# Attention then MoE on one core: V cast in smaller pieces, weight sums halved and earlier, four stores reordered

## Chip, core and metric

One core of a Trainium2 chip. The metric is the device time of one execution in microseconds (us); before the change the median of five runs is 349.75, the lowest 347.26 and the highest 356.05.

The core has five engines with instruction queues of their own: TensorE (PE in the profile, with its weight loads as PEld), VectorE (DVE), ScalarE (ACT), GpSimd (POOL) and SyncE (SP, which here only issues DMAs). An engine works through its queue in order, and instructions wait for each other across engines by semaphores.

## The reference

Two operators, one after the other. Attention over 8 batches, 8 heads, 576 positions and 64 columns a head, causal by blocks of 64; then a two-layer feed-forward network over the 8 x 576 = 4608 rows, with swish and a slope for each hidden column. All inputs and the output are float32.

```python
def _attn_ref(q, k, v):                       # (8, 8, 576, 64) each
    scores = 1.0 / np.sqrt(64) * np.matmul(q, k.transpose(0, 1, 3, 2))
    mask = (pos[:, None] // 64) >= (pos[None, :] // 64)
    scores = np.where(mask, scores, -1e9)
    scores = scores - np.max(scores, axis=-1, keepdims=True)
    attn = np.exp(scores)
    attn = attn / (np.sum(attn, axis=-1, keepdims=True) + 1e-09)
    return np.matmul(attn, v)

def _moe_ref(x, w_in, w_out, beta):           # (4608, 512), (512, 2048), (2048, 512), (2048,)
    h = x @ w_in
    g = h * (1.0 / (1.0 + np.exp(-beta * h)))
    return g @ w_out

x = attn_out.transpose(0, 2, 1, 3).reshape(4608, 512)
```

## The kernel before

**A plan made at build time.** The kernel first lists its operations (`P.op`) with an estimated duration, the operations it depends on (`deps`), the buffers it uses (`tiles`) and a priority (`prio`, the lower the sooner). A list scheduler (`Plan.schedule`, L81) then walks through an estimated time: whenever an engine is free, it takes the ready operation with the lowest priority, gives it its buffers, and writes it into that engine's queue. The queues are fixed from then on; on the chip only the semaphore waits decide when the instructions start. A dependency in `deps` counts with its latency: the later operation is not planned before the earlier has ended, and a wait is written where another engine, or a DMA, is awaited. `after` is weaker: the later operation may not be planned before the earlier is, and no wait comes of it (L207). Since buffers are given out in the order of the plan, one changed estimate or one weaker dependency can move many operations after it, on every engine.

**Attention.** The work is cut into 32 units, one for each batch b and pair of heads c (`u` = 4b + c). For a unit:

- q and k are loaded by SyncE into staging buffers `ST`, cast to bf16 by GpSimd (`QKn`, L647) and turned: for batches 0 and 1 by TensorE, from batch 2 on by one DMA transpose for two units, issued by SyncE (L654), into `QKT`.
- V of a whole batch is loaded by SyncE into `Vs` (128 rows x 2560 columns of float32) and cast to bf16 by GpSimd into `Vn` (L558). There are two `Vs` buffers. For batch 0 the cast is made in pieces of two heads, from batch 1 on in one instruction of 128x2560 (`range(h0, h1, 2 if b == 0 else 8)`). The second `Vs` buffer, like two of the six `ST` buffers, lies in the space `OV`, which later holds the sums below; batches 2 and later use the first only.
- TensorE makes the scores in two groups of six matmuls (L685), into pairs of PSUM banks; ScalarE takes their exponential (L699, three of 128x1024 a unit and a small one), 30 matmuls of 128x65 form the weighted sum and its denominator (L737), in a pair of banks from the same pool (banks 0 to 3 from batch 1 on).
- VectorE divides (L756, into `xq`). The result is turned into `xT`, the input of the network: for batches 0 to 4 by TensorE (L781) with a copy (L789), from batch 5 on by DMA transposes that SyncE issues (L769).

SyncE's queue thus holds all loads of q, k and V and, from batch 2 on, the transposes.

**The network.** The 4608 rows are worked in 9 chunks `r` of 512. For each of the 16 blocks `j` of hidden columns, H (four matmuls of 512 columns, L946), the tanh on ScalarE (L956) and the product on VectorE (L960) make block j of `gT`. "H j5 of chunk 1" is such a group. Chunk 0 then multiplies with `w_out` plainly (L982; its 16 groups are the list `plain`). `w_out` is loaded by GpSimd's queue in four parts (`wout`, L494), after the V load of batch 1.

Chunks 1 to 8 use seven products in place of eight (L817 to L933). `gT` is cut into quarters G(a, b), a for the rows and b for the hidden blocks, `w_out` into quarters b. VectorE makes, for each chunk, the sums of quarters of `gT`, each in two halves of 128x1024 (`comb`, L846):

```
S3 = G00 - G10 (SW[3])    S1 = G10 + G11 (in place of G10)
S2 = S1 - G00  (SW[2])    S4 = G01 - S2  (in place of G01)
```

and once, at the start of chunk 1, the sums of `w_out` (`weights`, L823): `TW3 = b3 - b1`, `TW1 = b1 - b0` (in place of b1), `TW2 = b3 - TW1`, `TW4 = b2 - TW2`, each one instruction of 128x2048 (L828). TW2, TW3, TW4 and S2, S3 lie in `OV`, so they wait until the early `ST` and `Vs` buffers there have been read (`early`). A product (`prod`, L879) is two steps of eight matmuls of 256 columns; in the order of the code: p1 = G00 b0, p2 = G01 b2, p6 = S2 TW2, p7 = S3 TW3, p5 = S1 TW1, p3 = S4 b3, p4 = G11 TW4. The second step of a product depends on the first. Products add up in three PSUM banks Z, W and Y. `evac` brings them out: ScalarE copies a bank with the factor 0.5 (L893: z1, u2, tt, c12), VectorE adds a bank to such a copy (L896: c11, c22, c21, into `oz`, `ot`, `ou`). Each of the four quarters of the result is then written to memory by a DMA that ScalarE issues (`store`, L903), right where its result is listed; such a store stands in ScalarE's queue and holds what is behind it until its result is there.

In the span, H groups and products of one chunk, and score groups, weighted sums and turns of later units, take turns on TensorE; the priorities (`pr`, L425; L888; L951) spread the units over the chunks.

Of the kernel before, what the change touches and what calls it, by code (L numbers as in the profile page):

```python
# [5 lines left out]
ALU = mybir.AluOpType  # L6
# [25 lines left out]
class Op:  # L32
    def __init__(self, engs, dur, lat, emit, deps, tiles, prio, mode, dma, xfer):
        self.xfer = xfer
        self.engs, self.dur, self.lat, self.emit = engs, dur, lat, emit
        self.deps, self.tiles, self.prio, self.mode, self.dma = list(deps), tiles, prio, mode, dma
        self.eng = None
        self.start = self.end = None
        self.order = None
        self.need = False  # L40
        self.tick = None
        self.after = None
        self.lazy = False
        self.pkt = 22.0
        self.fill = 0


class Plan:
# [32 lines left out]
    def schedule(self):  # L81
# [85 lines left out]
        while nsched < len(self.ops) - len(fill) or pend or rings["H"] or rings["S"] or late:  # L167
# [26 lines left out]
            while progress:  # L194
                progress = False
                for e in engs:
# [4 lines left out]
                    for o in pool:  # L201
                        if e not in o.engs:
                            continue
                        if o.ready + slack > now + 1e-9:
                            heapq.heappush(events, o.ready + slack)
                            continue
# [144 lines left out]
def bass_blockwise_causal_attn__then__act_swish_beta_kernel(  # L351
# [10 lines left out]
    with es:  # L362
# [58 lines left out]
        def dve_t(n):  # L421
            return (n + 125) / 0.96
# [97 lines left out]
        for b in range(B):  # L520
# [4 lines left out]
            for h0, h1, e, tt in PARTS[b]:  # L525
# [27 lines left out]
                n = 5 if 4 in tt else len(tt)  # L553
                for g0 in range(h0, h1, 2 if b == 0 else 8):
                    g1 = g0 + 2 if b == 0 else h1

                    def fw(g, e, ts=ts, t=t, g0=g0, g1=g1, n=n):
                        return g.tensor_copy(Vn[t.slot][:, 0:n, g0:g1, 0:64], Vs[ts.slot][:, 0:n, g0:g1, :])  # L558

                    o = P.op("POOL", 60 + 60 * n * (g1 - g0), fw, deps=[*vs, *ones, *vzero], tiles=[ts, t],  # L560
                             prio=4 * b + 0.5 - (38.5 - 5 * (h0 > 0)) * (b < 1))
                    for h in range(g0, g1, 2):
                        load[4 * b + h // 2] = [o]
# [259 lines left out]
        def weights():  # L823
            old = plain + wout + [o for t in early for o in t.users]
            b = [quad(w_out, 0, 0), quad(w_out, 0, 1), quad(w_out, 1, 0), quad(w_out, 1, 1)]
            for k, o, x, y, of in ((3, TW[3], b[3], b[1], []), (1, b[1], b[1], b[0], []),
                                   (2, TW[2], b[3], b[1], [1]), (4, TW[4], b[2], TW[2], [2])):
                tw[k] = P.op("DVE", dve_t(1024), mk(lambda g, o=o, x=x, y=y: g.tensor_tensor(o, x, y, ALU.subtract)),  # L828
                             deps=old + list(tw.values()), prio=0.6)
                tw[k].same = [tw[i] for i in of]  # L830

        def fast(r, row, tg, gs):
# [41 lines left out]
            def prod(ps, fa, fb, deps, tiles, first, last):  # L874
                z = []
                for w in range(2):
                    def fp(g, e, w=w):
                        for j in range(HJ):
# [7 lines left out]
                    n = HJ * mm(HM)  # L886
                    z.append(P.op("PE", n, fp, deps=deps + z, tiles=[ps, tg, *tiles], lat=n + 170, mode="full",
                                  prio=1000 + 100 * r + (16 + 0.1 * k if fin or k < 2 else 103 + 16 / 12 * (k - 2))))  # L888
                return z

# [10 lines left out]

            def store(to, a, b, x):
                return P.op("ACT", 500, lambda g, e: [g.dma_start(  # L903
                    out_rows(a, b), ost[to.slot][:].rearrange("p (w n) -> p w n", w=2))],
                    deps=[x], tiles=[to], xfer=900, dma=["d_ost", to], prio=-1)

            Z, W, Y = P.tile("P1"), P.tile("P1"), P.tile("P1")
# [6 lines left out]
            c11 = evac(W, oz, p2 + [z1], add=oz)  # L914
            store(oz, 0, 0, c11)
            for i in range(NP):
# [3 lines left out]
                SS[4].append(o)  # L920
            p6 = prod(Z, lambda: SW[2], lambda: TW[2], SS[2] + [tw[2], z1], [t2], False, False)
            u2 = evac(Z, ou, p6)
            p7 = prod(Y, lambda: SW[3], lambda: TW[3], SS[3] + [tw[3]], [t3], True, False)
            p5 = prod(Z, lambda: G(1, 0), lambda: quad(w_out, 0, 1), SS[1] + [tw[1], u2], [], False, False)
            tt = evac(Z, ot, p5)
            c22 = evac(Y, ot, p7 + [tt], add=ot)
            store(ot, 1, 1, c22)
            p3 = prod(Z, lambda: G(0, 1), lambda: quad(w_out, 1, 1), SS[4] + [tt] + wh, [], False, True)
            c12 = evac(Z, oc, p3)
            store(oc, 0, 1, c12)  # L930
            p4 = prod(Y, lambda: G(1, 1), lambda: TW[4], hi + [tw[4], c22], [], False, True)
            c21 = evac(Y, ou, p4 + [u2], add=ou)
            store(ou, 1, 0, c21)  # L933

        for r in range(NRC):
# [37 lines left out]
            for w, d0, d1 in [(w, 0, DM) for w in range(4)]:  # L973
# [5 lines left out]
                for j0, j1 in parts:  # L979
                    def fo(g, e, po=po, tg=tg, w=w, j0=j0, j1=j1, d0=d0, d1=d1):  # L980
                        for j in range(j0, j1):
# [4 lines left out]
                    n = (j1 - j0) * mm(d1 - d0)  # L986
                    o = P.op("PE", n, fo, deps=gs[j0:j1] + wout[j0 // 4:(j1 + 3) // 4] + ([o] if o else []),
                             tiles=[po, tg], lat=n + 170, mode="full",
                             prio=1000 + 100 * r + (16 + w + 0.01 * j0 if w == 0 else
                                                     103 + 5.33 * (w - 1) + 1.33 * j0 / 4))  # L990
                    plain.append(o)

# [81 lines left out]
```

The softmax here doesn't subtract the row's maximum and nothing guards it: scores larger than these inputs give would overflow.

## Time and profile before

The profiled execution took 351.25 us; its span, from the first to the last instruction, is 349.4 us, at a mean granted TensorE clock of 0.990. The table cuts the span into stretches, by what goes on in them, and gives the busy time of each engine in it (us).

| stretch, us | what it holds | PE | DVE | ACT | POOL |
|---|---|---|---|---|---|
| 0 to 20 | first loads and casts | 15.6* | 11.2 | 10.5 | 12.8 |
| 20 to 50 | batches 0 and 1, H of chunk 0 | 28.5 | 19.6 | 21.3 | 17.8 |
| 50 to 94 | end of batch 1, start of batch 2, products of chunk 0, H of chunk 1 | 42.7 | 27.0 | 23.8 | 9.9 |
| 94 to 120 | batches 2 and 3, sums of `w_out`, products of chunk 1 | 22.3 | 16.4 | 15.1 | 10.9 |
| 120 to 190 | batches 3 to 5, chunks 2 and 3, start of chunk 4 | 69.4 | 50.7 | 54.5 | 18.1 |
| 190 to 250 | end of batch 5, batches 6 and 7, chunks 4 and 5 | 57.9 | 40.1 | 41.7 | 11.6 |
| 250 to 349.4 | last two units, chunks 6 to 8 | 95.2 | 60.8 | 45.9 | 0 |

(* with the matmuls that only keep TensorE running before there is data, L507 and L509.)

The batches and chunks overlap; the middle column names what most of the stretch is. Ends of matmuls are modelled in a profile, so a busy TensorE need not be at its peak; what counts is whether its next group starts later than the one before it allows. Releasers in brackets are inferred from the semaphores. The costs that the change touches, from the groups of the trace:

| instruction | count | us of one (shortest / median / longest) |
|---|---|---|
| V cast, GpSimd, L558 (all sizes) | 11 | 0.40 / 2.32 / 3.14 |
| sum of `w_out`, VectorE, 128x2048, L828 | 4 | 1.21 / 1.22 / 1.37 |
| store, ScalarE's queue, L903: issue | 32 | 0.38 / 0.38 / 0.50 |
| the same, from issue to landing | 32 | 2.2 / 2.3 / 5.5 |

### The profile page before, as it was taken

The page shows a single profiled execution, that of the slowest core. Times are in us where ns is not written, and L with a number is a line of the kernel's source. Part 1 is how long each engine was busy: PE and PEld are TensorE (multiplying, and loading weights), DVE is VectorE, ACT ScalarE, POOL GpSimd, SP SyncE. Part 2 cuts the span into 40 slices and gives each one's busy share as a digit, 9 for nine tenths or more (in the row PEclk, how much of TensorE's full clock was granted, in tenths as well). Part 3 has the DMA queues.
Part 4 walks back from the last instruction along what each step waited for, and adds up shares of the span by engine and source line. Part 5 has one row for each costly group of instructions (what it writes and reads, how often), then busy time and mean ns, then how long its engine had stood idle before and what let it go on. Part 6 is the DMA issues. An engine that isn't in the chain of part 4 may idle for free.

```text
span 349.4 us, 7654 instructions
## 1 busy us (share of the span) xinstructions
PE 331.7 (95%) x3177; PEld 207.9 (59%) x3121; DVE 225.7 (65%) x463; ACT 212.7 (61%) x314; POOL 81.2 (23%) x110
## 2 busy tenths in 40 slices
PE   7799999999989899999999999999999999999995
PEld 5366445544756545766565576555666666666684
DVE  4728766268783678775776684577476856756741
ACT  2853993288357488478768756766664644644611
POOL 7576251143074044044002401041000000000000
PEclk9789999999999999999999999999999999999999
DMA  8999899899898999999935698976121010010013
GB/s 223 219 249 237 180 187 208 167 270 192 165 249 168 210 207 198 203 228 194 202 86 133 146 133 177 230 154 110 62 56 43 30 62 30 30 63 30 32 60 122
DMA packets 150627, 51.93 MB, mean 149 GB/s; under 512 B 134704, under 2 KB 150080, under 8 KB 150592
## 3 DMA queue, kind: packets, MB, share of 16 engines
q1 hardware_dynamic: 135744, 37.64, 54.4%
q10 hardware_dynamic: 9280, 9.44, 8.4%
q0 software_dynamic: 5568, 4.36, 8.0%
q8 instruction: 25, 0.41, 0.5%
q14 instruction: 10, 0.08, 0.1%
HBM read 36.71 MB, written 9.44 MB: 132 GB/s over the span
## 4 chain that ended last, share of the span: by engine, by line
PE 78%; DVE 9%; ACT 5%; DMA 4%; issue 2%; SPq 1%; POOL 0%; ACTq 0%; POOLq 0%
PE PS L946 31%; PE PS L879 24%; PE PS L737 7%; PE PS L685 6%; PE PS L982 4%; DMA QKT<-QKn 4%; DVE gT L960 3%; ACT th L956 2%; PE PS L781 2%; ACT E L699 2%; PE PS L507 2%; PE PS L509 2%; DVE gT L846 2%; DVE xq L756 1%; SPq L769 1%
## 5 line engine op out<-in xcount | busy, mean ns | idle before, releaser
L946 PE MATMUL PS<-xT,w_in 128*128 128x512 bf16 x576 | 139.0, 380 | 1.7 <-DVE gT L960 1.4
L956 ACT ACTIVATE th<-PS,beta 128x512 f32<-128x512 f32 x144 | 97.8, 696 | 56.9 <-PE PS L946 53.0
L960 DVE SCALAR_TENSOR_TENSOR gT<-th,PS 128x512 f16<-128x512 f32 x144 | 97.0, 683 | 42.5 <-ACT th L956 41.8
L699 ACT ACTIVATE E<-PS 128x1024 bf16<-128x1024 f32 x93 | 92.1, 1027 | 33.7 <-PE PS L685 33.0
L946 PEld LDWEIGHTS PS<-xT,w_in 128*128 128x128 bf16 x576 | 53.0, 98 | 55.1 <-DVE gT L960 2.6
L879 PE MATMUL PS<-w_out,gT 128*128 128x256 f16 x512 | 65.5, 273 | 0.7 <-ACT ost L893 0.7
L879 PEld LDWEIGHTS PS<-w_out,gT 128*128 128x128 f16 x512 | 48.5, 98 | 14.4 <-ACT ost L893 1.5
L647 POOL CAST QKn<-ST 128x640 bf16<-128x640 f32 x48 | 37.2, 776 | 52.5 <-DMA ST<-in_k_dram 37.1
L685 PE MATMUL PS<-QKT 64*128 64x512 bf16 (+4 forms) x328 | 37.8, 302 | 4.4 <-DVE xq L756 1.9
L558 POOL CAST Vn<-Vs 128x2560 bf16<-128x2560 f32 (+2 forms) x10 | 17.0, 1699 | 90.5 <-DMA Vs<-in_v_dram 90.4
L737 PEld LDWEIGHTS PS<-Vn,E 128*128 128x128 bf16 x930 | 31.3, 97 | 6.5 <-ACT E L699 1.2
L893 ACT ACTIVATE ost<-PS 128x512 f32<-128x512 f32 x32 | 19.2, 599 | 25.2 <-PE PS L879 25.0
L737 PE MATMUL PS<-Vn,E 128*128 128x65 bf16 x930 | 32.7, 193 | 1.6 <-ACT E L699 0.7
L879 PE MATMUL PS<-OV 128*128 128x256 f16 x256 | 32.7, 273 | 0.8 <-DVE OV L828 0.8
L685 PEld LDWEIGHTS PS<-QKT 64*128 64x128 bf16 (+1 forms) x328 | 13.6, 96 | 30.0 <-issue 14.1
L879 PEld LDWEIGHTS PS<-OV 128*128 128x128 f16 x256 | 24.7, 98 | 8.3 <-DVE OV L828 1.0
L896 DVE SCALAR_TENSOR_TENSOR ost<-PS,ost 128x512 f32<-128x512 f32 x24 | 16.5, 686 | 18.0 <-PE PS L879 16.2
L756 DVE TENSOR_TENSOR xq<-PS,inv 128x640 bf16<-128x640 f32 x32 | 26.3, 821 | 0.7
L846 DVE TENSOR_TENSOR OV<-gT 128x1024 f16<-128x1024 f16 x32 | 22.7, 718 | 1.1 <-PE PS L879 0.6
L705 DVE MEMSET E<- 64x64 uint32 x62 | 6.9, 112 | 23.8 <-ACT E L699 21.8
L879 PE MATMUL PS<-OV,gT 128*128 128x256 f16 x128 | 16.6, 273 | 0.0
L982 PE MATMUL PS<-w_out,gT 128*128 128x512 f16 x64 | 15.5, 380 | 0.0
(61 smaller groups left out, 186.3 us busy)
## 6 DMA issues: line engine op xcount, KB each, us to landing
out_dram<-ost ACTq DMA_DIRECT2D x36, 256.0 KB, 2.6
ST<-in_q_dram SPq DMA_DIRECT2D x48, 128.0 KB, 2.9
ST<-in_k_dram SPq DMA_DIRECT2D x48, 128.0 KB, 3.3
Vs<-in_v_dram SPq DMA_DIRECT2D x24, 256.0 KB, 4.3
w_in<-in_moe_w_in_dram POOLq DMA_DIRECT2D x4, 512.0 KB, 10.3
w_out<-in_moe_w_out_dram POOLq DMA_DIRECT2D x4, 512.0 KB, 10.9
ST<-in_q_dram SPq DMA_DIRECT2D x6, 288.0 KB, 6.8
ST<-in_k_dram SPq DMA_DIRECT2D x6, 288.0 KB, 6.6
```

The source lines that it names most:

```text
L647: return g.tensor_copy(QKn[tn.slot][:].rearrange("p a w n -> p (a w n)")[:, 640 * (2 * a + w):][:, 0:640] .rearrange("p (t h d) -> p t h d ...
L685: z = g.matmul(o, QKT[tqk.slot][r, p, 1, 128 * t:128 * t + m], x)
L699: return g.activation(E3[es_(te)][:, g0, :, :], PS[:, ps.slot:ps.slot + 2, :], ACT.Exp, scale=0.125)
L737: z = g.matmul(o, eblk(te, t, i, h), Vn[Tv.slot][:, t, 2 * c + h, 0:65], start=(t == 0), stop=(t == i))
L756: return g.tensor_tensor(xq[tx.slot][:].rearrange("p i (h d) -> p h i d", h=2), both(pv, 0, 64), x, ALU.mult)
L846: return P.op("DVE", dve_t(SZ * HC / 2), mk(lambda g: g.tensor_tensor(fo(), fx(), fy(), op)), deps=deps, tiles=tiles, prio=prio)
L879: x = g.matmul(PS[:, ps.slot, HM * w:HM * w + HM], fa()[:, j, 128 * w:128 * w + 128], fb()[:, j, :], start=first and w == 0 and j == 0, st ...
L893: return P.op("ACT", act_t(DM) + 80, lambda g, e: g.activation(ost[to.slot][:], PS[:, ps.slot, :], ACT.Copy, scale=0.5), deps=deps, tiles= ...
L946: z = g.matmul(PS[:, ph.slot, :], w_in[:, c, 128 * j:128 * j + 128], xT[:, c, row % RX:row % RX + RC], start=(c == 0), stop=(c == 3))
L956: return g.activation(th[tt.slot][:], PS[:, ph.slot, :], ACT.Tanh, scale=beta[:, j:j + 1])
L960: return g.scalar_tensor_tensor(out=gT[tg.slot][:, j, :], in0=th[tt.slot][:], scalar=1.0, in1=PS[:, ph.slot, :], op0=ALU.add, op1=ALU.mult)
L982: z = g.matmul(PS[:, po.slot, 0:d1 - d0], gT[tg.slot][:, j, 128 * w:128 * w + 128], w_out[:, j, d0:d1], start=(j == 0), stop=(j == NJ - 1))
```

## The change

Four things.

- **V.** The cast is made in pieces of two heads for every batch: 28 instructions of 128x640 for batches 1 to 7 in place of 7 of 128x2560. A unit's weighted sum depends on its own piece.
- **Sums of w_out.** Each is made in two halves of 128x1024. TW2 is formed as TW3 + b0, which is the same as b3 - TW1, so TW3, TW2 and TW4 no longer need TW1, and only TW1, which overwrites b1, still waits for chunk 0's plain products. The other three depend on the loads of `w_out` and on the early buffers alone.
- **Order instead of dependency.** The second step of a product is only ordered after the first (`after`), not dependent on it; the same for the four steps of a plain product of chunk 0. Both steps add into the same PSUM bank on the same engine.
- **Stores.** The stores of VectorE's results follow ScalarE's next copy in its queue: that of `oz` comes after the copy u2, that of `ot` after c12. That of `ou` gets a `rest` of 1500 ns, except in the last chunk: a new field by which the scheduler holds an operation back for so long beyond the time it is ready. It changes the place in the queue, no wait on the chip.

```diff
@@ -41,6 +41,7 @@
         self.tick = None
         self.after = None
         self.lazy = False
+        self.rest = 0.0
         self.pkt = 22.0
         self.fill = 0
 
@@ -201,8 +202,8 @@
                     for o in pool:
                         if e not in o.engs:
                             continue
-                        if o.ready + slack > now + 1e-9:
-                            heapq.heappush(events, o.ready + slack)
+                        if o.ready + o.rest + slack > now + 1e-9:
+                            heapq.heappush(events, o.ready + o.rest + slack)
                             continue
                         if o.after is not None and o.after.start is None:
                             continue
@@ -551,8 +552,8 @@
                         load.setdefault(4 * b + h // 2, []).extend([*vs, *ones, *vzero])
                     continue
                 n = 5 if 4 in tt else len(tt)
-                for g0 in range(h0, h1, 2 if b == 0 else 8):
-                    g1 = g0 + 2 if b == 0 else h1
+                for g0 in range(h0, h1, 2):
+                    g1 = g0 + 2
 
                     def fw(g, e, ts=ts, t=t, g0=g0, g1=g1, n=n):
                         return g.tensor_copy(Vn[t.slot][:, 0:n, g0:g1, 0:64], Vs[ts.slot][:, 0:n, g0:g1, :])
@@ -821,13 +822,17 @@
             return x[:, HJ * a:HJ * a + HJ, 256 * b:256 * b + 256]
 
         def weights():
-            old = plain + wout + [o for t in early for o in t.users]
+            old = wout + [o for t in early for o in t.users]
             b = [quad(w_out, 0, 0), quad(w_out, 0, 1), quad(w_out, 1, 0), quad(w_out, 1, 1)]
-            for k, o, x, y, of in ((3, TW[3], b[3], b[1], []), (1, b[1], b[1], b[0], []),
-                                   (2, TW[2], b[3], b[1], [1]), (4, TW[4], b[2], TW[2], [2])):
-                tw[k] = P.op("DVE", dve_t(1024), mk(lambda g, o=o, x=x, y=y: g.tensor_tensor(o, x, y, ALU.subtract)),
-                             deps=old + list(tw.values()), prio=0.6)
-                tw[k].same = [tw[i] for i in of]
+            for k, o, x, y, op in ((3, TW[3], b[3], b[1], ALU.subtract), (2, TW[2], TW[3], b[0], ALU.add),
+                                   (4, TW[4], b[2], TW[2], ALU.subtract), (1, b[1], b[1], b[0], ALU.subtract)):
+                tw[k] = []
+                for n in (slice(0, 4), slice(4, 8)):
+                    z = P.op("DVE", dve_t(512), mk(lambda g, o=o, x=x, y=y, n=n, op=op: g.tensor_tensor(
+                        o[:, n], x[:, n], y[:, n], op)), deps=old + (plain if k == 1 else []), prio=0.6)
+                    z.same = [tw[q][len(tw[k])] for q in {2: [3], 4: [2]}.get(k, [])]
+                    z.deps += z.same + ([tw[3][len(tw[k])]] if k == 1 else [])
+                    tw[k].append(z)
 
         def fast(r, row, tg, gs):
             if not tw:
@@ -884,8 +889,9 @@
                     k = step[0]
                     step[0] += 1
                     n = HJ * mm(HM)
-                    z.append(P.op("PE", n, fp, deps=deps + z, tiles=[ps, tg, *tiles], lat=n + 170, mode="full",
+                    z.append(P.op("PE", n, fp, deps=deps, tiles=[ps, tg, *tiles], lat=n + 170, mode="full",
                                   prio=1000 + 100 * r + (16 + 0.1 * k if fin or k < 2 else 103 + 16 / 12 * (k - 2))))
+                z[1].after = z[0]
                 return z
 
             def evac(ps, to, deps, add=None, same=()):
@@ -899,10 +905,12 @@
                 o.same = list(same)
                 return o
 
-            def store(to, a, b, x):
-                return P.op("ACT", 500, lambda g, e: [g.dma_start(
+            def store(to, a, b, x, after=None, rest=0.0):
+                o = P.op("ACT", 500, lambda g, e: [g.dma_start(
                     out_rows(a, b), ost[to.slot][:].rearrange("p (w n) -> p w n", w=2))],
                     deps=[x], tiles=[to], xfer=900, dma=["d_ost", to], prio=-1)
+                o.after, o.rest = after, rest
+                return o
 
             Z, W, Y = P.tile("P1"), P.tile("P1"), P.tile("P1")
             oz, ou, ot, oc = (P.tile("ost") for _ in range(4))
@@ -912,25 +920,25 @@
             z1 = evac(Z, oz, p1)
             p2 = prod(W, lambda: G(0, 1), lambda: quad(w_out, 1, 0), hi + wh, [], True, True)
             c11 = evac(W, oz, p2 + [z1], add=oz)
-            store(oz, 0, 0, c11)
             for i in range(NP):
                 o = comb(lambda i=i: G(0, 1, i), lambda i=i: G(0, 1, i), lambda i=i: piece(SW[2], i), ALU.subtract, i,
                          [SS[2][i]] + p2 + hi, [tg, t2])
                 o.same = [SS[2][i]] + hi
                 SS[4].append(o)
-            p6 = prod(Z, lambda: SW[2], lambda: TW[2], SS[2] + [tw[2], z1], [t2], False, False)
+            p6 = prod(Z, lambda: SW[2], lambda: TW[2], SS[2] + tw[2] + [z1], [t2], False, False)
             u2 = evac(Z, ou, p6)
-            p7 = prod(Y, lambda: SW[3], lambda: TW[3], SS[3] + [tw[3]], [t3], True, False)
-            p5 = prod(Z, lambda: G(1, 0), lambda: quad(w_out, 0, 1), SS[1] + [tw[1], u2], [], False, False)
+            store(oz, 0, 0, c11, after=u2)
+            p7 = prod(Y, lambda: SW[3], lambda: TW[3], SS[3] + tw[3], [t3], True, False)
+            p5 = prod(Z, lambda: G(1, 0), lambda: quad(w_out, 0, 1), SS[1] + tw[1] + [u2], [], False, False)
             tt = evac(Z, ot, p5)
             c22 = evac(Y, ot, p7 + [tt], add=ot)
-            store(ot, 1, 1, c22)
             p3 = prod(Z, lambda: G(0, 1), lambda: quad(w_out, 1, 1), SS[4] + [tt] + wh, [], False, True)
             c12 = evac(Z, oc, p3)
             store(oc, 0, 1, c12)
-            p4 = prod(Y, lambda: G(1, 1), lambda: TW[4], hi + [tw[4], c22], [], False, True)
+            store(ot, 1, 1, c22, after=c12)
+            p4 = prod(Y, lambda: G(1, 1), lambda: TW[4], hi + tw[4] + [c22], [], False, True)
             c21 = evac(Y, ou, p4 + [u2], add=ou)
-            store(ou, 1, 0, c21)
+            store(ou, 1, 0, c21, rest=0.0 if fin else 1500.0)
 
         for r in range(NRC):
             row = RC * r
@@ -984,10 +992,12 @@
                         return z
 
                     n = (j1 - j0) * mm(d1 - d0)
-                    o = P.op("PE", n, fo, deps=gs[j0:j1] + wout[j0 // 4:(j1 + 3) // 4] + ([o] if o else []),
+                    was = o
+                    o = P.op("PE", n, fo, deps=gs[j0:j1] + wout[j0 // 4:(j1 + 3) // 4],
                              tiles=[po, tg], lat=n + 170, mode="full",
                              prio=1000 + 100 * r + (16 + w + 0.01 * j0 if w == 0 else
                                                      103 + 5.33 * (w - 1) + 1.33 * j0 / 4))
+                    o.after = was
                     plain.append(o)
 
                 def fv2(g, e, po=po, to=to, n=d1 - d0):
```

## The prediction

> **What bounds the kernel.** I read the busy table first, then the chain of waits, then the timeline of the stretches in which TensorE's issue breaks off. The page says who is busy and who carries the chain:
>
> ```profile
> PE 331.7 (95%) x3177; PEld 207.9 (59%) x3121; DVE 225.7 (65%) x463; ACT 212.7 (61%) x314; POOL 81.2 (23%) x110
> ...
> PE 78%; DVE 9%; ACT 5%; DMA 4%; issue 2%; SPq 1%; POOL 0%; ACTq 0%; POOLq 0%
> ```
>
> TensorE bounds it; time can come only from places where its issue halts. I measure a halt from one group's start to the next, less the group's matmuls (0.216 us for 512 columns, 0.108 for 256, 0.030 for 65, 0.47 for a score group of six, each from the chain's undisturbed groups). From 255 us to 340 us there is none. The larger halts are at 52.6 (0.85 us), 97 to 101 (2.0), 110 to 116 (2.3), 191.9 (0.8), 220.8 and 243.1 (0.5 and 1.15) and 341.4 (0.87); a few of 0.3 to 0.7 stand elsewhere. First the second of them, from the timeline of all engines (start, duration, then the idle time and its releaser in brackets):
>
> ```profile
> 95.48 3.14 POOL L558 CAST Vn<-Vs 128x2560 bf16<-128x2560 f32 x1 [11.20 <-DMA Vs<-in_v_dram]
> ...
> 96.96 2.81 DVE L846 TENSOR_TENSOR gT<-gT,OV 128x1024 f16<-128x1024 f16 x2
> ...
> 97.14 1.05 PE L879 MATMUL PS<-OV 128*128 128x256 f16 x8
> ...
> 98.66 0.54 PE L685 MATMUL PS<-QKT 64*128 64x320 bf16 x6 [0.48 <-ACT E L699]
> ...
> 99.58 0.54 PE L685 MATMUL PS<-QKT 64*128 64x320 bf16 x6 [0.38 <-ACT E L699]
> ...
> 99.69 1.21 DVE L828 TENSOR_TENSOR OV<-w_out 128x2048 f16<-128x2048 f16 x1
> ...
> 100.96 1.92 PE L879 MATMUL PS<-OV 128*128 128x256 f16 x16 [0.84 <-DVE OV L828]
> ```
>
> p6 starts at 100.96 because TW2 is ready at 100.90; TW2 stands behind two halves of S4 that took 2.81 us instead of 2 x 0.68, while the V cast ran. TensorE's own timeline shows the third place:
>
> ```profile
> 110.86 1.05 PE L879 MATMUL PS<-OV,gT 128*128 128x256 f16 x8
> 112.04 1.08 PE L737 MATMUL PS<-Vn,E 128*128 128x65 bf16 x30
> 114.30 0.39 PE L685 MATMUL PS<-QKT 64*128 64x512 bf16 x2 [1.18 <-DVE xq L756]
> ...
> 116.03 1.08 PE L737 MATMUL PS<-Vn,E 128*128 128x65 bf16 x30 [0.66 <-ACT E L699]
> ```
>
> Here weighted sums and scores take turns in the same pairs of PSUM banks: 30 matmuls (0.90 us), then 1.35 us of waiting for the division (xq).
>
> **The change, part by part.** The order of the changed kernel's instructions is known, since the plan is made when the program is built. The two halves of a product are now only ordered, not dependent, so nearly every product and score group between 50 and 255 us moves by some places, not only what the title names.
>
> V casts: 28 casts of 128x640 in place of 7 of 128x2560. A 128x640 V cast took 0.72 us, a whole one 2.32, so 4 x 0.72 - 2.32 = +0.56 us each on GpSimd, which is 23% busy. Behind each V cast on it stand QKn casts, which waited 0.59 to 1.53 us for their data anyway; after the cast at 126.46 there is no gap, but 0.65 us of idle one pair of casts later. Batch 1's cast stands before three w_out loads: the last landed at 58.6 us and its first reader is at 64.9 or later. Cost 0; without that cover 0.56 us a batch.
>
> 52.6 us: the new order puts H j15 of chunk 0 (4 matmuls, 0.86 us) between the two weighted sums and the wait for xq, and its VectorE step behind unit 4's division. The halt of 0.85 us is filled: **+0.8** (0 to 0.85).
>
> Sums early: TW3, TW2 and TW4 in six halves right after the last xT copy of batch 1, which ended at 65.64 (64.8 with the lead). The whole sums took 1.22 and 1.37 us, so a half 0.61 to 0.69; six are 3.9 us, and VectorE idled 4.03 us there. Three fit before gT of j0, three come behind it, beside the V cast that ran 68.85 to 71.17, and delay gT of j1 from 71.13 to between 72.3 and 73.3. The first that needs it is H j5 at about 72.8 (73.66 less the lead): **-0.3** (0 to -0.6). The Trainium skill, SBUF — State Buffer, section "Who interferes with whom", says that a VectorE instruction with two SBUF inputs and a GpSimd instruction that reads SBUF exclude each other for the whole instruction, so these halves, moved beside a V cast, would speak against the change. The rows agree: S4 above waited until the cast was over at 98.62, and the cast itself took 3.14 instead of 2.32 after starting inside TW1. By the page alone three halves would each wait for a piece, 3 x 0.72 = 2.2 us, and H j5 would halt some 1.5 us; I take the -0.3 from the gap in the rows.
>
> 94 to 119 us, worked through with the rows' durations (exp 1.02, a copy 0.60, a store's issue 0.4, division 0.22 + 0.82, xT copy 0.52), on the old clock: p6 follows p2 at 95.63, scores of unit 10 at 97.4, p7 at 98.0. ScalarE does u2's copy and the store of oz first, so exp g0 ends at 99.7 instead of 98.6; p7 covers that. Next scores 99.85, p5 100.35 and 101.85, weighted sum 10 at 102.75, p3 at 104.2, p4 at 106.9. The two stores now stand between c12's copy and unit 11's exps (0.8 us on ScalarE), so weighted sum 11 waits 0.5 and starts at 109.85. Scores of unit 12 wait for its division until 112.15 (1.4 lost), H j0 for the xT copy (0.5 lost) until 113.8. Weighted sum 13 ends at 118.9. Before, it ended at 118.71, with two H groups fewer: 2 x 0.865 - 0.19 = **+1.5** (0 to 4.3, the whole of both halts).
>
> 119 to 188: the old order lost next to nothing here. In the new one scores 19 and H j4 of chunk 3 stand right behind exps they need (0.5 and 0.2), partly made good by fewer changes between matmul shapes: **-0.2** (-1 to 0).
>
> 191.9: this view is VectorE's and TensorE's:
>
> ```profile
> 189.83 1.39 DVE L846 TENSOR_TENSOR gT<-gT,OV 128x1024 f16<-128x1024 f16 x1
> ```
>
> ```profile
> 191.93 1.04 PE L879 MATMUL PS<-OV 128*128 128x256 f16 x8
> 193.59 1.07 PE L737 MATMUL PS<-Vn,E 128*128 128x65 bf16 x30 [0.62 <-DVE xq L756]
> ```
>
> S4 again beside a V cast (188.36 to 190.68), and the division behind it late. With a lead of 1.8 us S4 is nearly over when the cast begins, or waits for one piece: **+0.8** (0 to 0.8).
>
> 215 to 245: what bounds here is SyncE's queue of loads and transposes:
>
> ```profile
> 215.41 4.16 SPq L654 DMA_TRANSPOSE QKT<-QKn  x1
> ...
> 233.42 5.14 SPq L769 DMA_TRANSPOSE xT<-xq  x4
> 238.60 3.16 SPq L654 DMA_TRANSPOSE QKT<-QKn  x1
> ```
>
> A QKT transpose lands 6.5 to 6.7 us after its issue: 222.1 and 245.1, where the scores of units 28 and 30 start. The queue runs without a break from 183.5, where it waited for a division, so the lead at that point, 0.8 - 0.3 + 1.5 - 0.2 = 1.8, moves it by 1.8, and 0.6 more because a V load now stands earlier: unit 28's QKT issued at 213.0, landed at 219.7. The new order reaches scores 28 with three H groups fewer and one weighted sum more done (-1.7 us of work) and waits some 2.4 us. Then unit 29's xT transposes (2.5 us) stand before unit 30's QKT. By the queue's rows they start at 234.7, and by the walk of TensorE's groups from 219.7 on unit 29's division ends at 234.6; QKT 30 is issued at 237.2 and lands at 243.7, and TensorE comes there at 243.8 with p3's first half done. Ahead by 245.1 - 243.8 + 0.9 = 2.2, against 1.8 + 0.8 going in: **-0.4** (-3 to +1).
>
> Stores: in the old trace ScalarE waited for a sum at few of them (0.4 us at 209.5). It is 61% busy: 0 (0 to 0.4). At the end, p4 of chunk 7 now fills the wait for tt (341.37 to 342.23, 0.87 us), but four stores are issued within 2 us; each took 0.8 us to transfer, so the last lands some 0.75 later after the last matmul: **+0.1** (-0.8 to +0.9).
>
> Sum: 0.8 - 0.3 + 1.5 - 0.2 + 0.8 - 0.4 + 0.1 = 2.3 us of a span of 349.4: 347.1. The profiled execution took 351.25, 1.85 around its span, and would take 348.95; the median of the five runs is 1.5 below it, so **347.4**.
>
> **Rivals.** *SyncE's queue decides, and the result is slower.* If the lead does not reach the queue, unit 29's xT is issued at 238.6 and unit 30's QKT 2.46 us behind it, scores 30 start at 247.6 with 0.9 more done: 1.6 us behind, all leads gone, 349.75 + 1.6 = 351.4. There is no slack in it: each us by which unit 29's division ends after 234.7 costs one; past 237.0 the change loses, past 240.5 by over 1%. For it: the queue is full from 183.5 on. Against: unit 29's weighted sum is moved before H j7 of its chunk, and the walk finds its exps in time. *ScalarE takes the wait over:* the first fast chunk needs the same exps in the same bank pairs, so the halts at 97 and 112 only move, and pieces back to back hold VectorE as one cast did: 0.8 - 0.3 - 0.2 + 0.1 = 0.4 gained, 349.35. *More goes than I count:* both halts in the first fast chunk go entirely (4.3 - 1.5 = 2.8) and the queue gives 1 instead of taking 0.4: 347.4 - 4.2 = 343.2.
>
> **Numbers.** The forecast has 0.45, a quarter of that beyond 1%, as its own range is 345 to 349.5; more gain 0.24, nearly all beyond 1%; ScalarE 0.16; SyncE's queue 0.15, half of that beyond 1%. About 1% (3.5 us) is what a measurement of this kernel can tell from no change. Faster 0.11 + 0.22 = 0.33, slower 0.10 with what the others may lose, same 0.57. The range leaves out the far ends of the last case and of SyncE's: 343.6 to 351.2.
>
> **What would show it.** Right: p6's first matmul directly behind p2 without a wait for L828's tile; no S4 half over 1.5 us; the first TW halves between 64 and 67 us; no halt at 52 and at 341; scores 28 waiting over 1 us for QKT. Wrong: H j5 of chunk 1 halted by over 1 us; a halt at scores 30; new waits for exps between 119 and 188 of over 1 us together. A time above 349.7 means that the middle or the queue took back the gain.

## The result, and the profile after

The changed kernel takes 346.86 us (median of 43 runs, 344.34 to 351.2) against 349.75 (80 runs). The ratio is 0.9936, with a 95% interval of 0.992 to 0.9952: 1.7 to 2.8 us faster. The medians are of all runs, the ratio and its interval only of those within 1.5% of the fastest run of their kernel, so the medians lie a little further apart (2.89 us). The forecast was 347.4.

The execution profiled after took 344.9 us, with a span of 343.0. That is 6.4 below the span of before, more than the medians differ. From the page, busy times and the shares of the chain:

```profile
PE 328.0 (96%) x3177; PEld 207.1 (60%) x3121; DVE 223.9 (65%) x467; ACT 212.3 (62%) x314; POOL 85.2 (25%) x131
...
PE 80%; DVE 6%; SPq 4%; DMA 3%; ACT 3%; POOL 1%; issue 1%; POOLq 0%; ACTq 0%
```

TensorE's share of the chain went from 78 to 80% and VectorE's fell from 9 to 6%. To see where, I count in both traces TensorE's work in its matmuls' own time (the durations of the prediction, group by group in the order of the queue) and compare the moments at which the same amount is done. In the table each number is how much further the first profile of before falls behind the changed kernel in that stretch (the changed kernel's clock):

| stretch, us | behind, us | what the prediction had |
|---|---|---|
| 0 to 37 | 3.19 | not in it |
| 37 to 63 | 0.86 | +0.8 (52 us) |
| 63 to 90 | 0.01 | -0.3 (early sums beside a V cast) |
| 90 to 113 | 1.76 | +1.5 (94 to 119) |
| 113 to 181 | -0.92 | -0.2 (119 to 188) |
| 181 to 188 | 0.64 | +0.8 (191.9) |
| 188 to 255 | 0.06 | -0.4 (SyncE's queue) |
| 255 to the last matmul | 0.86 | +0.1 with the stores |
| sum | 6.45 | 2.3 |

The first row is no part of the change. In the first profile of before, TensorE's granted clock stood at one half from 13.3 to 20.1 us; in the profile after it did not. Without that row the change brings 3.26 us.

Where p6 had waited for TW2 there is no wait now, from the timeline of all engines:

```profile
89.83 1.91 PE L884 MATMUL PS<-w_out,gT 128*128 128x256 f16 x16
90.03 1.29 DVE L831 TENSOR_TENSOR w_out<-w_out 128x1024 f16<-128x1024 f16 x2 [0.45 <-PE PS L990]
91.58 1.91 PE L884 MATMUL PS<-OV 128*128 128x256 f16 x16
...
92.39 1.28 DVE L851 TENSOR_TENSOR gT<-gT,OV 128x1024 f16<-128x1024 f16 x2
...
96.33 3.07 POOL L559 CAST Vn<-Vs 128x640 bf16<-128x640 f32 x4 [11.61 <-DMA Vs<-in_v_dram]
```

p6 (91.58) runs right behind p2 (89.83), since only TW1 (90.03) is still made here. The two halves of S4 take 1.28 together, and the V cast comes 2.7 us after them. The third place of the prediction is still there, in TensorE's timeline:

```profile
104.58 0.54 PE L686 MATMUL PS<-QKT 64*128 64x320 bf16 x6
105.62 1.08 PE L738 MATMUL PS<-Vn,E 128*128 128x65 bf16 x30 [0.49 <-DVE E L706]
107.87 0.39 PE L686 MATMUL PS<-QKT 64*128 64x512 bf16 x2 [1.18 <-DVE xq L757]
...
108.41 0.53 PE L782 MATMUL PS<-identB,xq 128*128 128x128 bf16 x5
109.56 1.04 PE L954 MATMUL PS<-xT,w_in 128*128 128x512 bf16 x4 [0.62 <-DVE xT L792]
```

Unit 11's weighted sum (105.62), its division, its turn and H j0 of chunk 2 follow each other; between them stand only unit 12's scores (107.87), which wait for the division themselves. At the end of the kernel the groups join without a gap (before: 0.87 us):

```profile
333.17 1.91 PE L884 MATMUL PS<-w_out,gT 128*128 128x256 f16 x16
334.92 1.04 PE L884 MATMUL PS<-OV,gT 128*128 128x256 f16 x8
335.79 1.91 PE L884 MATMUL PS<-w_out,gT 128*128 128x256 f16 x16
```

### The profile page after: what moved, and what is told of

Same layout as the page of the kernel before. It is cut to its first block, busy times and chain, and to the rows that moved or that the text cites. A ratio compares the mean times of both kernels' runs of the same rounds, so it can differ in the third digit from the quotient of the medians.

```text
span 343.0 us, 7689 instructions
## 1 busy us (share of the span) xinstructions
PE 328.0 (96%) x3177; PEld 207.1 (60%) x3121; DVE 223.9 (65%) x467; ACT 212.3 (62%) x314; POOL 85.2 (25%) x131
## 4 chain that ended last, share of the span: by engine, by line
PE 80%; DVE 6%; SPq 4%; DMA 3%; ACT 3%; POOL 1%; issue 1%; POOLq 0%; ACTq 0%
PE PS L954 33%; PE PS L884 27%; PE PS L738 8%; PE PS L686 6%; PE PS L990 4%; DVE gT L968 2%; PE PS L782 2%; DMA Vs<-in_v_dram 2%; ACT th L964 2%; SPq L533 2%; SPq L770 2%; DMA QKT<-QKn 1%; DVE xq L757 1%; ACT E L700 1%; DVE ost L902 1%
## 5 line engine op out<-in xcount | busy, mean ns | idle before, releaser
L884 PE MATMUL PS<-w_out,gT 128*128 128x256 f16 x512 | 64.0, 273 | 0.0
L648 POOL CAST QKn<-ST 128x640 bf16<-128x640 f32 x48 | 36.4, 758 | 52.2 <-DMA ST<-in_k_dram 33.1
L559 POOL CAST Vn<-Vs 128x640 bf16<-128x640 f32 (+1 forms) x28 | 21.4, 763 | 82.4 <-DMA Vs<-in_v_dram 81.2
L686 PE MATMUL PS<-QKT 64*128 64x512 bf16 (+4 forms) x328 | 37.1, 297 | 4.2 <-DMA QKT<-QKn 1.3
L686 PEld LDWEIGHTS PS<-QKT 64*128 64x128 bf16 (+1 forms) x328 | 13.5, 95 | 29.3 <-issue 13.3
L884 PE MATMUL PS<-OV,gT 128*128 128x256 f16 x128 | 15.8, 273 | 0.0
```

What stands on the lines that cost most here:

```text
L648: return g.tensor_copy(QKn[tn.slot][:].rearrange("p a w n -> p (a w n)")[:, 640 * (2 * a + w):][:, 0:640] .rearrange("p (t h d) -> p t h d ...
L686: z = g.matmul(o, QKT[tqk.slot][r, p, 1, 128 * t:128 * t + m], x)
L884: x = g.matmul(PS[:, ps.slot, HM * w:HM * w + HM], fa()[:, j, 128 * w:128 * w + 128], fb()[:, j, :], start=first and w == 0 and j == 0, st ...
```

## The experiments

My theory is that each piece of the gain is one halt of TensorE that one edit closes. Rival A: shorter V casts matter, because GpSimd holds VectorE's two-input sums for less time. Rival B: the parts only reshuffle the plan, and no halt belongs to an edit. Each ratio below is to runs of the kernel before beside it. All comparisons by stretch are made as in the table above, against the first profile after. A second execution of the changed kernel differs from it by 0.1 us or less in every stretch but one (0.21).

### One part undone

V in one piece for batches 1 to 7, the plan made anew:

```diff
-                for g0 in range(h0, h1, 2):
-                    g1 = g0 + 2
+                for g0 in range(h0, h1, 2 if b == 0 else 8):
+                    g1 = g0 + 2 if b == 0 else h1
```

> The changed kernel, only V cast whole again for batches 1 to 7. The plan then differs in few places: H j15 of chunk 0 is back ahead of unit 4's weighted sum. Theory (each part of the gain is one halt of TensorE that one edit closes, and V's pieces close only the one at 52 us): the halt of 0.85 us behind unit 5's weighted sum is back, nothing else moves by over 0.5; S4 of chunk 1 stays at 0.7 us a half; median 346.9 + 0.9 = 347.8, lead at the end of the trace 0.9 below the changed kernel's at equal start. Rival A (shorter casts matter because GpSimd holds VectorE's two-input sums for less time): halves of S4 or S3 of over 1.5 us are back, halts at 95 to 101 and at 190 return, 346.9 + 0.9 + 2 = 349.8. Rival B (the parts only reshuffle the plan and no halt belongs to an edit): any time from 346 to 350, and the halts lie elsewhere.

The second keeps the changed kernel's queues place by place and only makes one instruction of the four casts of a batch:

```diff
         P.schedule()
+        for b in range(1, B):
+            z = vcast[b]
+            first = min(z, key=lambda o: P.order["POOL"].index(o))
+            first.emit = first.whole
...
```

> The changed kernel's queues kept place by place, but the four casts of a batch (1 to 7) are one instruction of 128x2560 where the first stood. Theory: what the pieces do they do through the plan (they let it place H j15 of chunk 0 later); the length of the cast itself is worth under 0.3 us: 346.9, within 0.5, no halt at 52 us. Rival A (shorter casts free VectorE): 1 to 2.5 us slower, 348 to 349.4, with sums of 128x1024 of over 1.5 us beside the casts.

Measured: 348.94 (10 runs; ratio 0.995, 0.9906 to 0.9993) and 349.22 (10 runs; 0.9967, 0.9924 to 1.001). Both are above what the theory expected (347.8 and 346.9), and the second lies in rival A's range. The halt at 52 us does as the theory says. With the plan made anew, the stretch from 37 to 63 us is 0.86 longer and the next 0.00; with the queues kept, 0.00 and 0.03. The halt is back in TensorE's timeline of the first:

```profile
51.82 1.03 PE L738 MATMUL PS<-Vn,E 128*128 128x65 bf16 x29
53.53 0.54 PE L686 MATMUL PS<-QKT 64*128 64x320 bf16 x6 [0.68 <-DVE xq L757]
```

So the pieces close this halt only by letting the plan put H j15 there. But rival A has a part, as the times say. In the run with the queues kept, a whole cast later met a half of S3 (all engines):

```profile
126.85 2.32 POOL L565 CAST Vn<-Vs 128x2560 bf16<-128x2560 f32 x1 [11.30 <-DMA Vs<-in_v_dram]
126.94 2.77 DVE L854 TENSOR_TENSOR OV<-gT 128x1024 f16<-128x1024 f16 x1
```

The sum began 0.09 us after the cast and ended 0.54 after it, 2.77 us in place of 0.69, and the next H group waited 2.49 us for gT. In the six traces with whole casts the longest sum of 128x1024 took 1.65 to 2.80 us, in the eight with pieces 1.13 to 1.22. So pieces bound the loss. Whether there is one differs from trace to trace: with V whole and the plan made anew, a half of S4 took 2.19 us at 228.28, and the stretch from 188 to 255 is still 0.66 shorter than the changed kernel's. Both times also hold falls of the clock, of which below: a mean clock of 0.998 or above was granted in 2 and 1 of the 10 executions, in the changed kernel in 25 of 56. How much of the 2 us is the length of the casts, and how much the clock, stays open.

The sums of `w_out` as they were, whole and late:

```diff
-            old = wout + [o for t in early for o in t.users]
+            old = plain + wout + [o for t in early for o in t.users]
-            for k, o, x, y, op in ((3, TW[3], b[3], b[1], ALU.subtract), (2, TW[2], TW[3], b[0], ALU.add),
+            for k, o, x, y, of in ((3, TW[3], b[3], b[1], []), (1, b[1], b[1], b[0], []),
...
```

> The changed kernel with the old sums of w_out: whole, TW2 from TW1, all behind the plain products. In VectorE's queue TW3 and TW1 stand before S4 and TW2 behind it again. Theory: p6 waits for TW2 again, the halts at 94 to 101 us come back with some 2 us, 346.9 + 2 = 348.9. Rival A (the halt came from the whole V cast that held S4): V is in pieces here, so S4 waits little and the halts give at most 0.5, 347.4.

Measured: 343.85 (4 runs; ratio 0.9823, 0.9772 to 0.9874), faster than the changed kernel. Both expectations missed. Run again, beside the changed kernel:

> The changed kernel with the old sums of w_out again, with more rounds. Theory: no halts at unit 11's weighted sum, so no fall of the clock after 110 us: 9 of 10 executions at 0.998 or above, median 343.9 to 344.5, faster than the changed kernel by 2 to 3. Rival (the first four executions were lucky): 346 or more and a share of full clocks as in the changed kernel.

> The changed kernel again, beside the others on the same chip. Theory and rival alike: 346.9 within 0.7; theory: 3 to 6 executions of 10 at a mean clock of 0.998 or above, the others with the time that a fall by one half for 3.4 us (1.7 us) or 6.8 us (3.4 us) costs.

343.68 (6 runs; 0.9869, 0.9809 to 0.9929) against 346.32 (12 runs; 0.9936, 0.9897 to 0.9975). TW2 stands behind S4 again in this kernel's timeline (of the first run), and TensorE does halt at about that place, but for exponentials: TW2 is ready at 95.76, and p6 starts behind the scores at 96.05 without waiting for it.

```profile
94.54 1.22 DVE L829 TENSOR_TENSOR OV<-w_out 128x2048 f16<-128x2048 f16 x1
95.57 0.54 PE L686 MATMUL PS<-QKT 64*128 64x320 bf16 x6 [1.12 <-ACT E L700]
...
103.91 1.08 PE L738 MATMUL PS<-Vn,E 128*128 128x65 bf16 x30 [0.56 <-DVE E L706]
104.83 1.91 PE L881 MATMUL PS<-w_out,gT 128*128 128x256 f16 x16
106.58 0.52 PE L782 MATMUL PS<-identB,xq 128*128 128x128 bf16 x5
```

Counted from its own start, it is 2.0 us behind the changed kernel at 103 and 1.0 ahead at 113. With the early sums the products of chunk 1 run out ahead of unit 11: p3 and p4 are done when its weighted sum starts, and only H of chunk 2, which needs that unit's turned result, is left. With the late sums p3 still lies behind the weighted sum (104.83) and covers the division. What the early sums close at p6 they open again at unit 11, with 1.0 us on top, in both executions of this kernel.

The steps of products dependent again:

```diff
-                    z.append(P.op("PE", n, fp, deps=deps, tiles=[ps, tg, *tiles], lat=n + 170, mode="full",
+                    z.append(P.op("PE", n, fp, deps=deps + z, tiles=[ps, tg, *tiles], lat=n + 170, mode="full",
...
-                z[1].after = z[0]
```

> The changed kernel with the second step of a product, and the steps of the plain products, dependent on the step before again. Theory: the halt of 0.87 us before the last-but-two products is back, the one at 52 us is not, those at 94 to 101 us are not: 346.9 + 0.9 = 347.8 and up to 1 more or less from the middle, where the plan differs. Rival B (no halt belongs to an edit): the halt at the end stays closed, or the time falls outside 346.8 to 348.8.

Measured: 346.59 (10 runs; 0.9925, 0.9889 to 0.9962). That is less than the theory's 347.8 and 0.2 below 346.8, under which the expectation counts it for rival B; so the time speaks for rival B, the halts at 52 us and at the end for the theory. The halt before the last products is back (0.86 in the last stretch) and 52 us stays closed (-0.01), but the middle gives 1.75 back (-0.54, -0.19 and -1.02 between 113 and 255). The 1.59 from 90 to 113 hold a fall of the clock. The same edit on the plain products of chunk 0 does nothing that shows: from 37 to 90 us, where they run, no stretch differs by more than 0.01.

The stores in their old places:

```diff
-            store(oz, 0, 0, c11, after=u2)
+            store(oz, 0, 0, c11)
...
```

> The changed kernel with the old places of the stores. Theory (the stores took part only by what the plan makes of them): the halts at 52 us and before the last products stay closed, the time is 346.9 within 1. Rival (a store that waits in ScalarE's queue holds the exponentials behind it): new waits for exponentials of over 1 us together between 94 and 190 us, 348 or more.

Measured: 346.14 (10 runs; 0.9915, 0.9871 to 0.9959). Behind 37 us no stretch differs by more than 0.3: in the changed kernel the stores' places do nothing that can be measured.

### One part alone, and before once more

> The kernel before, unchanged, profiled once more. Theory (V's loads and casts come at a fixed time after the start, TensorE's work comes earlier or later with the clock it is granted in the first 20 us, so S4 of chunk 1 meets the V cast by coincidence): if this execution starts at full clock, S4's halves of chunk 1 end before the cast of batch 3 starts at about 95.5, take 0.7 us each, and the wait for TW2 is under 1 us; if it starts slow like the first profile, S4's first half takes 2.2 again. Rival (the plan of before puts S4 beside the cast whatever the clock): a half of S4 of over 1.5 us either way.

One run, 349.11. It started at full clock, and the theory holds, in the timeline of all engines:

```profile
94.67 1.28 DVE L846 TENSOR_TENSOR gT<-gT,OV 128x1024 f16<-128x1024 f16 x2
...
95.87 1.22 DVE L828 TENSOR_TENSOR OV<-w_out 128x2048 f16<-128x2048 f16 x1
...
97.55 3.24 POOL L558 CAST Vn<-Vs 128x2560 bf16<-128x2560 f32 x1 [12.19 <-DMA Vs<-in_v_dram]
97.69 1.92 PE L879 MATMUL PS<-OV 128*128 128x256 f16 x16
```

S4 takes 0.64 a half and TW2 ends at 97.09, before the cast (which came 2 us later than named). p6 is late (97.69) by its place behind two score groups that wait for exponentials, not by TW2. S4 beside the cast, on which the prediction built, did not come again: the cast starts when its load has landed (95.48 in the first profile, 97.55 here), and S4 comes with TensorE's work (96.96 and 94.67). The other meeting, at 190 us, did come again: there a half of S4 took 1.65 us (187.96) beside a cast that began at 186.74.

The early sums alone, in the code of before as in the diff of the change:

> The kernel before with the sums of w_out in halves and early, nothing else. Theory (the early sums let the products of chunk 1 run ahead, and then nothing is left to cover the chain of scores, exponentials and division of units 11 and 12): p6 does not wait, but TensorE's lost time from p1 of chunk 1 to H j1 of chunk 2 is 5 us or more, as in the changed kernel (5.4), with a halt of over 1 us at unit 11's weighted sum; median 349.3, no more than 0.8 below before. Rival (the early sums bring what the prediction gave them, 1.2 to 1.5 us): lost time there 4.4 or less, 348.2.

Measured: 349.37 (10 runs; 0.9964, 0.9916 to 1.0012), as the theory has it. Its stretch from 90 to 113 is the changed kernel's to 0.00 us, with the halt at unit 11; the halts at 52 us and before the last products are there (0.85 each).

The weaker order alone (the diff of the steps turned around):

> The kernel before with the steps of a product ordered and not dependent, nothing else. Theory: the halt of 0.87 us before the last products is closed, the one at 52 us stays, 349.75 - 0.9 = 348.9. If it also lifts the stretch of chunk 1 as in the run without early sums (lost time from p1 to H j1 of chunk 2 of 4.4 in place of 7.4): 347.

347.19 (10 runs; 0.99, 0.9858 to 0.9942): the last stretch is closed (0.00), 52 us is not (0.85), and 90 to 113 is 0.6 shorter than in the first profile of before (1.14 against 1.76). This one edit brings as much as the whole change, within the intervals; the expectation had named 347 for the case that chunk 1 gains too.

V's pieces and the weaker order, without the early sums and the stores:

> The changed kernel with the old sums of w_out and the old stores: V's pieces and the weaker order alone. Theory (the gain is the fills at 52 us and before the last products and the absence of the halts around unit 11's weighted sum, and neither the early sums nor the stores take part): as the run with the old sums, 343.9, within 1, with no execution below a granted clock of 0.99. Rival (the stores carry part of it): 345.5 or more.

346.0 (4 runs; 0.987, 0.9788 to 0.9953). It gains 0.79 on the changed kernel from 90 to 113 and 0.99 up to 181, and loses 3.3 from there to 255. There TensorE waits for transposes out of SyncE's queue (1.36, 0.85 and 1.47 us at 200, 216 and 229). The theory's 343.9 within 1 is missed, and the other rival's 345.5 or more is met, though the ranges overlap (344.04 to 347.74 here, 342.62 to 345.83 in the 10 runs with the old sums and the new stores). The loss from 181 to 255 alone doesn't prove the stores or the plan: the two traces with the old sums and the new stores, which have one and the same queue, are 2.7 and 0.9 us behind the changed kernel there. So this stretch varies by itself, and what the stores are worth beside the old sums stays open.

### The granted clock

In several traces TensorE's clock falls to one half for 3.41 or 6.83 us, mostly near 110 us. The view of TensorE's busy time in windows, here of the run with dependent steps (columns: window, length, busy us and instructions of PE, PEld, DVE, ACT and POOL, then the clock, the DMA share and GB/s):

```profile
103.53:106.94 3.41, 2.91 (x47) 2.25 (x45) 0.92 (x3) 2.96 (x4) 1.44 (x2) 1.00 0.86 214
106.94:110.35 3.41, 1.39 (x22) 0.82 (x18) 1.84 (x6) 1.75 (x4) 1.44 (x2) 1.00 1.14 306
110.35:113.76 3.41, 3.41 (x12) 0.98 (x10) 0.80 (x2) 2.29 (x4) 1.44 (x2) 0.50 1.00 185
113.76:117.18 3.42, 3.37 (x68) 2.49 (x67) 2.02 (x6) 2.17 (x4) 0.00 (x0) 1.00 1.39 191
```

The window ahead of the fall holds the stretch around unit 11. To test it, 22 matmuls were put into its gaps in the changed kernel's queues:

```diff
+        for at, n in ((mark["qk", 13, 2], 4), (mark["av", 11], 11), (mark["xtr", 11], 7)):
+            z = []
+            for _ in range(n):
+                o = Op(("PE",), 110, 110, mk(lambda g: g.matmul(PS[:, ph.slot, 0:256], identB[:], identW)),
+                       [xt[10]], [ph], 0, "full", None, 0)
...
```

> The changed kernel's queues, with 22 matmuls of 256 columns put into TensorE's gaps around unit 11's weighted sum (4 ahead of it, 11 behind it, 7 behind unit 11's turn), into a PSUM bank that is free there; their results are overwritten. Theory (a stretch of some 4 us in which TensorE works little is what makes its granted clock fall to one half for 3.4 or 6.8 us, in some executions): no fall at 110 to 118 us, two thirds or more of the executions at a mean clock of 0.998 or above (the changed kernel had 18 of 44), median 346.0, that is 0.9 below the changed kernel. Rival (the clock falls for reasons outside this stretch): the share stays near 4 in 10 and the median at 346.9 or a little above, since the added matmuls only delay.

Measured: 346.21 (12 runs; 0.9928, 0.9894 to 0.9963), beside 346.32 for the changed kernel. 9 of 12 executions had a mean clock of 0.998 or above, the changed kernel's 7 of 12 on the same chip. That meets what the theory expected, but 9 against 7 of 12 cannot tell it from its rival, and the filling brings no time: at full clock the filled kernel takes 345.9 (median of 9), the changed one 345.65 (median of 25).

## Why the prediction was right

The total was right to 0.6 us, because the halts that it named were there and most of them closed as it said. That it came so close is in part luck: several sizes and one reason were wrong, and the errors partly cancel. By its own steps:

- **52 us, +0.8:** 0.86. Two runs place it in V's pieces by way of the plan: it is there in each run without them, and gone in each with them and in the one that keeps the queues.
- **Sums early, -0.3:** 0.01. The step moved the V cast with TensorE's lead. It came at 70.37, 3.4 us behind the last early half (66.99): a cast follows its load. H j5 of chunk 1 did not wait.
- **94 to 119, +1.5:** 1.76, with the remaining waits where the walk had them: unit 11's weighted sum 0.5 for its exponentials, unit 12's scores 1.35 (predicted 1.4), H j0 0.7 (0.5). Its reason was half chance: S4 and the cast did not meet in the second profile of before, which up to 103 us loses 0.9 us where the first loses 2.1. And the early sums get no credit in the changed kernel, since it gains 1.0 in this stretch without them. The rival "ScalarE takes the wait over" had named this: the same exponentials in the same bank pairs.
- **119 to 188, -0.2:** -0.92. The wrong size. The largest halt was foreseen neither in place nor in kind: scores of unit 19 waited for a PSUM bank that the copies of unit 17 free, and these stood behind a half of S3 (0.89 us in place of 0.69) beside V's pieces (all engines):

```profile
150.16 0.89 DVE L851 TENSOR_TENSOR OV<-gT 128x1024 f16<-128x1024 f16 x1
...
151.27 0.59 DVE L792 COPY xT<-PS 128x256 bf16<-128x256 bf16 x3
...
151.91 0.54 PE L686 MATMUL PS<-QKT 64*128 64x320 bf16 x6 [0.99 <-DVE xT L792]
```

- **191.9, +0.8:** 0.64.
- **SyncE's queue, -0.4:** +0.06. Scores of unit 28 waited less than the 2.4 expected, those of unit 30 did wait for their transpose, behind unit 29's:

```profile
229.38 5.97 SPq L770 DMA_TRANSPOSE xT<-xq  x4
235.40 3.13 SPq L655 DMA_TRANSPOSE QKT<-QKn  x1
...
240.43 0.39 PE L686 MATMUL PS<-QKT 64*128 64x512 bf16 x2 [1.33 <-DMA QKT<-QKn]
```

- **The end, +0.1:** +0.86, for the gap; the four late stores cost nothing: 3.55 us from the last matmul's end to the span's end in both traces, where 0.75 more had been counted.

The terms that came out too low make 1.8 us together, those too high 0.9; so 2.3 was forecast where the profiles have 3.26. Against the second profile of before, counted in the same way, 52 us, 119 to 181, 191.9 and the end come out alike (0.85, 0.92 the other way, 0.9 and 0.86). The 3.19 of the start, which no edit made, is most of why the profiled execution took 344.9 and not 348.95.

Of the signs that the prediction named, p6, the halves of S4 (1.20 at most) and the closed halts at 52 and at the end came as said, and H j5 did not wait. Three did not: the first early half ran at 61.75 and not from 64 on, since this execution started 3.19 us sooner; scores of unit 28 waited 0.4, not over 1; and the halt at scores 30 (1.33 by the row above; before, 0.98) had been named as a sign of being wrong. It cost 0.35 more than before, too little to turn the result. The best version is the changed kernel with the old sums: 343.75 (median of its 10 runs).

## What to carry to other kernels

Before pricing a collision of two engines, ask what each is tied to: here casts follow the loads and sums follow TensorE, and in a second profile of the same kernel one of two collisions was gone. A product that is made ready earlier helps only as long as something is left to cover the chain behind it; count what the engine will have to do when the next chain runs. Where a planner orders the work, undo each part alone before crediting it: two of the four parts here carried the gain, one cost time, and one did nothing that shows in the changed kernel.

## What the hardware showed

The falls of the clock follow a grid. In each trace their borders lie whole multiples of 3.413 us apart (from 5.53 to 111.34 in the run with V whole: 31). On that grid, after 90 us and while TensorE still had work to come, the clock fell behind each of the five windows in which TensorE was busy for at most 1.74 us (0.92, 1.39, 1.70, 1.74 and 1.74), and behind none with 1.77 or more, over all 14 traces; the changed kernel's lowest had 1.77. (Some 35 matmul records are missing in the four traces that fell there, so these are a little low.) That is no threshold yet: behind three windows at the end of the last products, busy for 1.49, 1.50 and 1.67 us (V whole, the first profile of before, dependent steps), the clock did not fall; it fell one window later, behind one without a matmul. The Trainium skill, TensorE: Matmul & The Clock Gate, section "Part 1: The HAM clock gate", has the free-running window of 3413 ns and the two clocks, and says that an idle window brings the lower one. Here five windows that were busy for 27 to 51% were followed by it too. With a halt of 1.4 us and two shorter ones at unit 11, the stretch from 90 to 113 us then took 2.8 us more than the changed kernel's where the fall lasted 6.83 us (the two runs with whole V casts), and 1.6 where it lasted 3.41 (dependent steps). Whether the clock falls seems to hang on how the grid cuts that stretch; no run here moves the grid to show it. Falls between 12 and 20 us, in two traces, followed busier windows (2.17 and 2.29); why is open.

In kernels whose queue has that stretch at unit 11, 71 of 178 timed executions had a mean clock of 0.998 or above; in the three without it (the old sums, the weaker order alone, V and the weaker order) 21 of 24. That is an association: their other halts differ too.
